# Sign bits of 27 weight chunks moved from VectorE to ScalarE and GpSimd, weight checks from step 60, two query tiles

## The chip, the cores and the metric

The kernel runs on one core of a Trainium2 chip (trn2). The engines of the core are called PE (TensorE: matmuls), DVE (VectorE), ACT (ScalarE), POOL (GpSimd) and SP (SyncE, which issues the transfers). Each engine works through its own queue of instructions in order and waits there on semaphores of the others. The metric is the time of one execution in device microseconds.

## The reference

Attention that keeps the 32 largest scores of each row, then two dense layer pairs on its output. Batch 4, 8 heads, 576 tokens, head size 64; widths 512 -> 1024 -> 512 -> 2048 -> 512.

```python
scores = scale * np.matmul(q, k.transpose(0, 1, 3, 2))
kth = np.partition(scores, -top_k, axis=-1)[..., -top_k:-top_k + 1]      # top_k = 32
scores = np.where(scores >= kth, scores, -1000000000.0)
attn = softmax(scores)                       # exp(s - max) / (sum + 1e-9)
x = (attn @ v) as [2304, 512]
...
h = x @ w_in                                 # moe_: 512 -> 1024
solu = h * softmax(h)
ln = (solu - mean) / np.sqrt(var + 1e-06) * g_ln
x2 = ln @ w_out                              # 1024 -> 512
...
h = x2 @ w_in                                # moe2_: 512 -> 2048
g = h * (1.0 / (1.0 + np.exp(-1.702 * h)))
return g @ w_out                             # 2048 -> 512
```

The weights, q, k and v come as 64-bit floating point numbers; the kernel reads them as pairs of 32-bit words.

## The kernel before, in words

Every matmul is made of three products of 16-bit parts (a value is split into a high and a low half, `PASSES`), so each operand that PE reads has been split before: ACT writes the high half, POOL or DVE the low half.

**Weights.** The four weight matrices are cut into 48 chunks of 128 x 512 (`CHUNKS`: 8 of the first matrix, 8 of the second, then alternately 4 of the third and 4 of the fourth for each of four groups g). They all live in one tile, `wt`, of 50 slots; a raw chunk takes two slots, and `w_loads` and `room` issue the next load on SP when slots ahead are free, up to 6 chunks ahead. `w_decode` (L210) makes a 32-bit float from the two words of each number with three DVE operations: L228 shifts the high word and masks it, L229 puts the sign bit back in, L230 adds the top bits of the low word. `w_split` (L255) then scales the chunk on ACT, writes the high half on ACT (L143, the helper that records every ACT operation) and the low half on POOL (L121). `DECODE` hands out 4 or 8 chunks at each of the first eight steps, in program order.

**Attention.** 72 steps, each with two heads of a block of 128 queries (18 blocks of queries come to the expert layers; there are 16 main blocks of four steps, and four tails of two). A step: `scores` on PE (L426, tile `sc`), `copy_s` on ACT, `fold` on DVE (L444 to L447), `rounds` on DVE (L455, L458: the eight largest, four times), `pick` on POOL (L468), `mask` (ACT, and POOL L476), `exp_of` and `high` on ACT, `low` on POOL (L494), `turn` (a transposing transfer on SP to the tile `et`), and three steps later `back` on PE (L577). The queries are prepared by `prep_q`, which fills one `qt` tile for each half of the heads of a block with a transposing transfer (L382) and two copies (L384); the pool holds three such tiles.

**Expert layers.** Each finished block goes through class `Block`: `a` (L681, PE, 24 matmuls), exponentials and normalisation into `zh`, `b` (L748), `x2_high` on ACT and `x2_low` on DVE (L764), and then for g = 0 to 3: `c` (L778, PE, into the one PSUM bank `m`), `tanh` (ACT, tile `t`), `gelu` (DVE, L787), `g_high` (ACT), `g_low` (POOL, L798), `d` (L805, PE, into the one PSUM bank `o`); at last `store` copies `o` to `y` on ACT. `t`, `y` and the `junk` tile of the weight checks share one pool tag with two buffers.

**Checks.** Sums of squares of all inputs are collected in `insq`; those of the weights are taken by `w_check` (L918, an ACT Square with a sum, one of 24 at each step from step `W_CHECK` = 20 on). Near the end of the program text `insq` is summed over the partitions on POOL (L1088, a custom instruction), and a flag made of all checks decides whether a slower exact version runs.

**Order.** The program text gives priorities. The order in which each engine's queue stands is made by a scheduler before the run, which puts instructions of later text ahead where it takes an engine to be free. So a change at one place moves instructions at others.

Of the kernel before, what the change touches and what calls it, by code (L numbers as in the profile page):

```python
# [1 line left out]

# [5 lines left out]
F32 = mybir.dt.float32  # L8
# [14 lines left out]
W_RAW = 6  # L23
W_STAGE = 4
TWO_BANKS = 32
LAG = 3
DECODE = (4, 4, 4, 4, 8, 8, 8, 8)
SLOTS = {6: 2, 7: 2}
FIRST_SLOT = 6
R_BUFS, EH_BUFS, QT_BUFS, GH_BUFS = 2, 2, 3, 3  # L30
TAIL_AT = (1,)
W_CHECK = 20
PIN_TO = -1
KV_BUFS, RAW_BUFS, S_BUFS, ET_BUFS = 4, 2, 3, 2
S_IN = 2.0 ** 8
S_EXP = 2.0 ** -19
S_Z = 2.0 ** 10
# [4 lines left out]
def attn_moe_kernel(tc: tile.TileContext, *args):  # L42

    nc = tc.nc
    with ExitStack() as ctx:
        flag = layers(ctx, tc, True, *args)
        again = nc.values_load(flag, min_val=0, max_val=1)
    with tc.If(again > 0):
        with ExitStack() as ctx:
            layers(ctx, tc, False, *args)  # L50


def in_order(tc, start, engines):
# [12 lines left out]
def layers(ctx, tc, quick, q, k, v, w1, w2, g_ln, w3, w4, out):  # L66
# [127 lines left out]
    def w_load(i):  # L194
# [8 lines left out]
        else:  # L203
            wraw[i] = []
            for z in range(2):
                t = ghp.tile([128, 256, 2], I32, tag="gh", name="wraw")
                nc.sync.dma_start(t.rearrange("p n a -> p (n a)"), words[:, z * 512:(z + 1) * 512])
                wraw[i].append(t)

    def w_decode(i):  # L210

        parts = wraw.pop(i)
        if not quick:
            f = wt[:, i + 1, :]
        else:
            at_f[i] = room(i + 1, 1, 0)
            f = wt[:, at_f[i], :]
            del at_raw[i]
        wraw[-1 - i] = f
        w = 512 // len(parts)  # L220
        for z, raw in enumerate(parts):
            lo, hi = raw[:, :, 0], raw[:, :, 1]
            fi = f[:, z * w:(z + 1) * w].bitcast(I32)
            ti = fi
            if quick:
                ti = (p_m.tile([128, 512], I32, tag="m", name="wi") if i % 2 and i < TWO_BANKS else
                      p_o.tile([128, 512], I32, tag="o", name="wi"))
            nc.vector.tensor_scalar(ti, hi, 3, 0x3FFFFFF8, op0=ALU.logical_shift_left, op1=ALU.bitwise_and)  # L228
            nc.vector.scalar_tensor_tensor(ti, hi, -0x40000000, ti, op0=ALU.bitwise_and, op1=ALU.bitwise_or)  # L229
            nc.vector.scalar_tensor_tensor(fi, lo, 29, ti, op0=ALU.logical_shift_right, op1=ALU.bitwise_or)  # L230
        if quick:
            return
        j, kc, cb = CHUNKS[i]
        if j == 1:
            act(f, f, AF.Copy, scale=gl[:, kc:kc + 1])
        junk = at.tile([128, 512], F32, tag="t", name="junk")
        act(junk, f, AF.Square, accum_out=wsq[:, i:i + 1])
# [17 lines left out]
    def w_split(i):  # L255
        j, kc, cb = CHUNKS[i]
        o = wview(i)
        if not quick:
            scale = wsc[:, j:j + 1]
        elif j == 1:  # L260
            scale = gl[:, kc:kc + 1]
        else:
            scale = S_W[j]
        split(wraw.pop(-1 - i), o[:, 0], o[:, 1], scale, "w")

    def w1v(kc, hl, half):
# [150 lines left out]
    def scores(blk, j):  # L417
        t = qt[blk][0]
        sc = p_sc.tile([128, 1536], F32, tag="sc", name="sc")
        for i in range(2):  # L420
            c0 = 0
            for c1 in ((MAIN, S) if i == 0 else (2 * MAIN - S, S)):
                for hl in range(2):
                    for rows, qi, kp, par in heads(blk, j, i):
                        k0 = par * 704
                        nc.tensor.matmul(sc[rows, i * S + c0:i * S + c1], t[qi // 4][:, hl, qi % 4, rows],  # L426
                                         kts[kp][:, k0 + c0:k0 + c1], start=(hl == 0), stop=(hl == 1))
                c0 = c1
        fr[(blk, j)] = [sc]

    def copy_s(blk, j):
        sc = fr[(blk, j)][0]
        s = sp.tile([128, 2, S], F32, tag="s", name="s")
        act(s.rearrange("p a n -> p (a n)"), sc[:, 0:2 * S])
        fr[(blk, j)].append(s)
# [42 lines left out]
    def exp_of(blk, j, i):  # L478
        s, pk = fr[(blk, j)]
        if j == 0 and i == 0:  # L480
            rsum[blk] = sm.tile([128, 8], F32, tag="rsum", name="rsum")
        rs = rsum[blk][:, 2 * j + i:2 * j + i + 1]
        act(s[:, i], s[:, i], AF.Exp, bias=pk[:, i, 1:2], scale=S_EXP, accum_out=rs)

    def high(blk, j):
        s = fr[(blk, j)][0]
        eh = ehp.tile([128, 2, 2 * S], F16, tag="eh", name="eh")
        act(eh[:, 0], s.rearrange("p a n -> p (a n)"))
        fr[(blk, j)] = [s, eh]
# [178 lines left out]
    class Block:  # L668
# [39 lines left out]

        def square(self):
            st_ = self.st  # L710
            self.zh = one.tile([128, 1024], F16, tag="zh", name="zh")
            self.dev = zsq[:, self.no:self.no + 1] if quick else st_[:, 5:6]
            act(self.zh, self.hf, AF.Square, bias=st_[:, 4:5], accum_out=self.dev)

# [213 lines left out]
    def w_loads(i, most=99):  # L928

        while wload[0] < min(WCH, i + 1 + W_RAW, most):  # L930
            j = wload[0]
            r = room(j, 2, max(1, min(W_STAGE, (WCH + SHIFT - j - 2) // 2)))
            if r is None:
                return
            at_raw[j] = r
            w_load(j)
            wload[0] += 1


    def decode(n):  # L940
        for _ in range(n):
            i = wnext[0]
            if i == WCH:
                return
            wnext[0] += 1
            w_decode(i)
            w_split(i)
            w_loads(i)


    last_kv = {}
# [21 lines left out]
    def load_for(t):  # L973
        for w in work.get(t, ()):
            gen = w[2](*w[3])
            next(gen)
            loaded.append(gen)
# [17 lines left out]

    def place(name):
        for f in slot.get(name, ()):
            f()

    t = 0  # L1000
    while True:
        count = 0 if t < FIRST_SLOT else SLOTS.get(t, 1)
        live = t < NS
        for z in range(max(count, 1)):
            slot = {}
            if z < count:
                place_no = len(at_step)
                at_step.append(t)
                while len(base) < len(queue) and (not base or place_no >= base[-1] + 5):
                    base.append(place_no - 1)  # L1010
                for m, b0 in enumerate(base):
                    for name, f in queue[m].at(place_no - b0).items():
                        slot.setdefault(name, []).append(f)
            on = live and z == 0
            if z == 0:
                if t + 1 < NS:
                    scores(*steps[t + 1])
                load_for(t + 1)
                if 1 <= t <= NS:
                    exp_of(*steps[t - 1], 0)  # L1020
                    exp_of(*steps[t - 1], 1)
                    high(*steps[t - 1])
                if t + 1 < NS:
                    copy_s(*steps[t + 1])
                if 1 <= t <= NS:
                    low(*steps[t - 1], 0)
                    low(*steps[t - 1], 1)
                    turn(*steps[t - 1])
                if LAG <= t < NS + LAG:
                    back(*steps[t - LAG])  # L1030
            place("gh")
            place("c")
            place("early")
            if on:
                rounds(*steps[t], (0,))
            place("dve1")
            if on:
                rounds(*steps[t], (1,))
            place("dve2")
            place("tanh")  # L1040
            if on:
                rounds(*steps[t], (2, 3))
                pick(*steps[t])
            place("dve3")
            place("gl")
            place("mid")
            if on:
                mask(*steps[t])
            place("big")
            place("d")  # L1050
            if z == 0 and t + 1 < NS:
                fold(*steps[t + 1])
            place("gelu")
            if z == 0 and LAG <= t < NS + LAG and ends(t - LAG):
                finish(steps[t - LAG][0])
            place("last")
            place("late")
            if z < count - 1 and t < len(DECODE):
                decode(DECODE[t] // count)
        if live:  # L1060
            for w in work.get(t, ()):
                run(loaded.pop(0))
            if t < len(DECODE):
                decode(DECODE[t] - (DECODE[t] // max(count, 1)) * (max(count, 1) - 1))
            if t >= W_CHECK and t - W_CHECK < WCH // 2:
                w_check(t - W_CHECK)
        t += 1
        if t == PIN_TO:
            in_order(tc, start, ("DVE",))
        if len(base) == NBLK and len(at_step) > base[-1] + 13:  # L1070
            break
# [59 lines left out]
```

## Time and profile before

| what | value |
|---|---|
| median of 3 runs | 989.79 us (986.56 to 990.15) |
| profiled execution, its own time | 986.16 us |
| its span, first to last instruction | 984.3 us |
| granted TensorE clock, mean | 0.913 |
| busy: PE, DVE, ACT, POOL | 760.7, 777.0, 709.7, 667.2 us |

No engine is busy for the whole span, since the parts of the program have different limits; the profile is best read by stretches of time. "Idle before" in a row is the time that the engine did nothing ahead of the instruction, and the name behind the arrow is what ended that; "issue" means that the profile shows nothing that it waited for.

### The profile page before, as it was taken

What the parts mean: (1) busy time and instruction counts of PE and PEld (TensorE: products, weight loads), DVE (VectorE), ACT (ScalarE), POOL (GpSimd) and SP (SyncE); (2) the same over time, 40 slices, a digit from 0 to 9 for tenths busy, and PEclk for the clock granted to TensorE, in tenths of its full rate; (3) what the DMA queues carried; (4) which work ended last, traced back from release to release, by engine and by line L of the source; (5) the groups of instructions that cost most, each with busy time, mean ns of one, the idle gap of its engine ahead of it and who ended that gap; (6) DMA issues with size and microseconds to landing.
All of it is one profiled execution on the core that took longest, in us unless ns stands there. A gap on an engine that the chain in (4) does not pass through costs nothing. (4 is left out here: it accounts for less than half of the span.)

```text
span 984.3 us, 22216 instructions
## 1 busy us (share of the span) xinstructions
PE 760.7 (77%) x8224; PEld 490.6 (50%) x8224; DVE 777.0 (79%) x2197; ACT 709.7 (72%) x1230; POOL 667.2 (68%) x673
## 2 busy tenths in 40 slices
PE   1223434644849999998899999898879999999995
PEld 0112222422525766665565665575546666666563
DVE  4999999989887898897887998798769999621220
ACT  4688777678877888889899977879478777722321
POOL 1477767659786588777788886878588877733311
PEclk9995657867778999999899999999979999999998
DMA  6998757567864477667686666757555745642200
GB/s 156 284 290 196 193 130 183 113 135 153 195 133 89 82 130 129 102 124 137 118 140 132 107 123 114 146 120 121 107 102 104 130 86 93 105 68 33 43 23 16
DMA packets 337734, 122.67 MB, mean 125 GB/s; under 512 B 315344, under 2 KB 329168, under 8 KB 337616
## 3 DMA queue, kind: packets, MB, share of 16 engines
q1 hardware_dynamic: 337616, 121.16, 59.9%
q8 instruction: 66, 1.08, 0.4%
q14 instruction: 52, 0.43, 0.1%
HBM read 39.85 MB, written 4.72 MB: 45 GB/s over the span
## 5 line engine op out<-in xcount | busy, mean ns | idle before, releaser
L455 DVE MAX8 wk<-wk 128x8 f32<-128x296 f32 x576 | 240.6, 455 | 0.0
L778 PE MATMUL h<-x2t,wt 128*128 128x128 f16 x3456 | 209.7, 221 | 14.1 <-ACT wt L143 4.6
L494 POOL TENSOR_TENSOR eh<-s,eh 128x576 f16<-128x576 f32 x144 | 181.3, 1281 | 51.9 <-ACT eh L143 32.9
L778 PEld LDWEIGHTS <-wt 128*128 128x128 f16 x3456 | 199.7, 99 | 21.9 <-issue 6.3
L476 POOL TENSOR_TENSOR s<-s,r 128x576 f32<-128x576 f32 x144 | 181.7, 1281 | 42.0 <-ACT r L143 41.8
L805 PE MATMUL o<-wt,gh 128*128 128x512 f16 x864 | 202.3, 383 | 5.7 <-DVE wt L230 3.7
L458 DVE MATCH_REPLACE8 wk<-wk 128x296 f32<-128x296 f32 x432 | 192.0, 451 | 0.0
L577 PE MATMUL av<-vt,et 128*128 128x64 f16 (+1 forms) x2400 | 91.7, 204 | 90.9 <-DMA et<-eh 82.8
L426 PE MATMUL sc<-kt,qt 128*128 128x64 f16 (+7 forms) x640 | 97.9, 320 | 76.2 <-DVE wk L447 52.7
L577 PEld LDWEIGHTS <-et 128*128 128x128 f16 (+1 forms) x2400 | 83.4, 108 | 106.1 <-DMA et<-eh 95.9
L805 PEld LDWEIGHTS <-gh 128*128 128x128 f16 x864 | 83.3, 99 | 100.1 <-issue 10.5
L798 POOL TENSOR_TENSOR gh<-t,gh 128x512 f16<-128x512 f32 x72 | 83.4, 1160 | 71.6 <-ACT gh L143 70.9
L143 ACT ACTIVATE r<-s,picks 128x576 bf16<-128x576 f32 x144 | 103.5, 765 | 31.9 <-POOL picks L468 31.5
L143 ACT ACTIVATE s<-s,picks 128x576 f32<-128x576 f32 x144 | 110.4, 767 | 22.1 <-POOL s L476 21.9
L787 DVE SCALAR_TENSOR_TENSOR t<-t,h 128x512 f32<-128x512 f32 x72 | 48.7, 677 | 90.6 <-ACT t L143 90.2
L748 PE MATMUL x<-wt,zt 128*128 128x512 f16 x432 | 105.8, 399 | 15.4 <-DMA zt<-zh 14.9
L426 PEld LDWEIGHTS <-qt 128*128 128x128 f16 (+1 forms) x640 | 48.4, 109 | 125.7 <-DVE wk L447 42.1
L681 PE MATMUL ha<-wt,xt 128*128 128x512 f16 x432 | 102.6, 396 | 10.3 <-DVE x2hl L764 10.3
L143 ACT ACTIVATE s<-sc 128x1152 f32<-128x1152 f32 x72 | 80.3, 1116 | 17.7 <-PE sc L426 12.7
L143 ACT ACTIVATE t<-h 128x512 f32<-128x512 f32 x72 | 42.1, 585 | 65.2 <-PE h L778 60.0
L143 ACT ACTIVATE eh<-s 128x1152 f16<-128x1152 f32 x72 | 83.1, 1154 | 0.7
L444 DVE TENSOR_TENSOR wk<-sc,s 128x576 f32<-128x576 f32 x72 | 54.1, 751 | 34.3 <-ACT s L143 30.3
(79 smaller groups left out, 1043.7 us busy)
## 6 DMA issues: line engine op xcount, KB each, us to landing
wt<-in_moe_w_in_dram SPq DMA_DIRECT2D x24, 512.0 KB, 5.2
wt<-in_moe_w_out_dram SPq DMA_DIRECT2D x24, 512.0 KB, 4.6
qt<-qt SPq DMA_DIRECT2D x72, 64.0 KB, 2.0
raw<-in_k_dram SPq DMA_DIRECT2D x32, 128.0 KB, 2.8
raw<-in_q_dram SPq DMA_DIRECT2D x16, 256.0 KB, 3.3
vraw<-in_v_dram SPq DMA_DIRECT2D x32, 128.0 KB, 2.6
out_dram<-y SPq DMA_DIRECT2D x16, 256.0 KB, 2.4
et<-eh SPq DMA_TRANSPOSE x72, 4.8
```

The lines of the kernel that those rows point to most:

```text
L143: nc.scalar.activation(out, in_, func, **kw)
L426: nc.tensor.matmul(sc[rows, i * S + c0:i * S + c1], t[qi // 4][:, hl, qi % 4, rows], kts[kp][:, k0 + c0:k0 + c1], start=(hl == 0), stop=(h ...
L455: nc.vector.max(out=wk[:, i, at_:at_ + 8], in_=wk[:, i, 0:W_END])
L458: nc.vector.match_replace(out=wk[:, i, 0:W_END], in_to_replace=wk[:, i, at_:at_ + 8], in_values=wk[:, i, 0:W_END], imm_value=LOW)
L476: nc.gpsimd.tensor_tensor(s[:, i], s[:, i], r[i], op=ALU.subtract)
L494: nc.gpsimd.tensor_tensor(eh[:, 1, cols], s[:, i], eh[:, 0, cols], op=ALU.subtract)
L577: nc.tensor.matmul(o[rows, col:col + 64], et[:, ea, 4 * i + c, rows], vts[kp][:, va, vc:vc + 64], start=(n == 0), stop=(n == 14))
L681: nc.tensor.matmul(h[:, half * 512:half * 512 + 512], self.xt[:, a, kc], w1v(kc, w, half), start=(n == 0), stop=(n == 11))
L748: nc.tensor.matmul(self.x2, self.zt[:, a, kc], w2v(kc, w), start=(n == 0), stop=(n == 23))
L778: nc.tensor.matmul(h2[:, mm * 128:(mm + 1) * 128], w3v(kc, w, 4 * g + mm), self.x2t[:, a, kc], start=(n == 0), stop=(n == 11))
L798: nc.gpsimd.tensor_tensor(gh[:, 1], t.rearrange("p (a n) -> p a n", a=4), gh[:, 0], op=ALU.subtract)
L805: nc.tensor.matmul(self.o, gh[:, a, mm], w4v(4 * g + mm, w), start=(g == 0 and n == 0), stop=(g == 3 and n == 11))
```

## The change

- Of the 40 chunks of the first, third and fourth matrix, two of three (27: those whose number is not 2 modulo 3) are decoded differently (`signed`). DVE shifts the high word and flips a bit in one operation, L229 is left out, and L230 follows. ACT takes the Sign of the raw high word into the slot of the chunk's high half; in `w_split` ACT's scaling copy becomes an Abs with the same scale, and POOL multiplies the result by the sign. The split into halves follows as before.
- The weight checks start at step 60 and go on after the last attention step.
- The pool of query tiles has two buffers in place of three. `zh` takes the buffer of `xt` in place of one of its own. The 4 KB per partition that this frees are not used.
- `HP_W`, `HP_MOE`, `HP_AT` and `DELAY` are new switches, all 0: `urgent` then does nothing.

```diff
+HP_W = 0
+SIGNED = (1, 1, 0)
+HP_MOE = 0
+DELAY = 0
+HP_AT = 0
...
-R_BUFS, EH_BUFS, QT_BUFS, GH_BUFS = 2, 2, 3, 3
+R_BUFS = 2
+EH_BUFS = 2
+QT_BUFS = 2
+GH_BUFS = 3
...
-W_CHECK = 20
+W_CHECK = 60
...
+def urgent(tc, offset):
+    return tc.high_priority(offset) if offset else nullcontext()
...
+    def signed(i):
+        return quick and CHUNKS[i][0] != 1 and SIGNED[i % len(SIGNED)]
...
-            nc.vector.tensor_scalar(ti, hi, 3, 0x3FFFFFF8, op0=ALU.logical_shift_left, op1=ALU.bitwise_and)
-            nc.vector.scalar_tensor_tensor(ti, hi, -0x40000000, ti, op0=ALU.bitwise_and, op1=ALU.bitwise_or)
+            if signed(i):
+                nc.vector.tensor_scalar(ti, hi, 3, -0x40000000, op0=ALU.logical_shift_left, op1=ALU.bitwise_xor)
+                act(wview(i)[:, 0], hi.bitcast(F32), AF.Sign)
+            else:
+                nc.vector.tensor_scalar(ti, hi, 3, 0x3FFFFFF8, op0=ALU.logical_shift_left, op1=ALU.bitwise_and)
+                nc.vector.scalar_tensor_tensor(ti, hi, -0x40000000, ti, op0=ALU.bitwise_and, op1=ALU.bitwise_or)
             nc.vector.scalar_tensor_tensor(fi, lo, 29, ti, op0=ALU.logical_shift_right, op1=ALU.bitwise_or)
...
+        elif not signed(i):
+            scale = S_W[j]
         else:
-            scale = S_W[j]
+            f = wraw[-1 - i]
+            act(f, f, AF.Abs, scale=S_W[j])
+            nc.gpsimd.tensor_tensor(f, f, o[:, 0], op=ALU.mult)
+            scale = None
         split(wraw.pop(-1 - i), o[:, 0], o[:, 1], scale, "w")
...
-            self.zh = one.tile([128, 1024], F16, tag="zh", name="zh")
+            self.zh = one.tile([128, 1024], F16, tag="xt", name="zh")
...
-            if t >= W_CHECK and t - W_CHECK < WCH // 2:
-                w_check(t - W_CHECK)
+        if W_CHECK <= t < W_CHECK + WCH // 2:
+            w_check(t - W_CHECK)
```

DVE's queue early in the program, where chunks 2 and 3 are decoded between the rounds of the first attention steps (L228 to L230 are the three decode operations), before:

```order
L228 TENSOR_SCALAR wi<-wt 128x512
L455 MAX wk<-wk 128x8 x2
L228 TENSOR_SCALAR wi<-wt 128x512
L229 SCALAR_TENSOR_TENSOR wi<-wt,wi 128x512
L458 MATCH_REPLACE wk<-wk 128x296 x2
L229 SCALAR_TENSOR_TENSOR wi<-wt,wi 128x512
L230 SCALAR_TENSOR_TENSOR wt<-wt,wi 128x512
```

The same place of the changed kernel, where L246 is the new first operation of a signed chunk and L249, L250 and L251 are the old three under new line numbers:

```order
L249 TENSOR_SCALAR wi<-wt 128x512
L481 MAX wk<-wk 128x8 x2
L246 TENSOR_SCALAR wi<-wt 128x512
L250 SCALAR_TENSOR_TENSOR wi<-wt,wi 128x512
L484 MATCH_REPLACE wk<-wk 128x296 x2
L251 SCALAR_TENSOR_TENSOR wt<-wt,wi 128x512 x2
```

Chunk 3 has two operations in place of three, and both chunks are finished one row earlier, ahead of what came between. Over the whole queue the last L230 stands behind 21 folds (L444) before and behind 19 in the changed kernel.

POOL's queue around the all-reduce of `insq` (L1088, with the rows marked ISA around it), before, where g_low of some block in the middle of attention comes ahead of it and a pick behind it:

```order
L476 TENSOR_TENSOR s_9152<-s_9152,r_9425 128x576
L798 TENSOR_TENSOR gh_9448<-t_9411,gh_9448 128x512
L1088 ISA
L1088 ISA tot_13436<-insq_75 128x56
L468 ISA
L468 TENSOR_TENSOR picks_73<-wk_9442,pickc_74 128x6
L121 TENSOR_TENSOR vt_10015<-vraw_9684,vt_10015 128x640
```

The all-reduce of the changed kernel (L1117 there, and L824 is g_low):

```order
L824 TENSOR_TENSOR gh_13079<-t_13037,gh_13079 128x512
L824 TENSOR_TENSOR gh_13153<-t_13134,gh_13153 128x512
L1117 ISA
L1117 ISA tot_13463<-insq_75 128x56
L824 ISA
L824 TENSOR_TENSOR gh_13222<-t_13206,gh_13222 128x512
L824 TENSOR_TENSOR gh_13291<-t_13275,gh_13291 128x512
L824 TENSOR_TENSOR gh_13362<-t_13345,gh_13362 128x512
L824 TENSOR_TENSOR gh_13429<-t_13413,gh_13429 128x512
```

It has moved from the middle of attention to the place ahead of the last four g_low of the program, those of the last block.

ACT's queue at the end of the program, before (`t` is a tanh, `gh` a g_high, `y` the copy of a block's output):

```order
L143 ACTIVATE t_13111<-h2_13060 128x512
L143 ACTIVATE gh_13130<-t_13111 128x512
L143 ACTIVATE t_13181<-h2_13132 128x512
L143 ACTIVATE gh_13197<-t_13181 128x512
L143 ACTIVATE t_13248<-h2_13199 128x512
L143 ACTIVATE y_13315,ysum_78<-o_13044 128x512
L143 ACTIVATE gh_13264<-t_13248 128x512
```

The same place of the changed kernel:

```order
L157 ACTIVATE t_13134<-h2_13083 128x512
L157 ACTIVATE junk_13154,insq_75<-wt_121 128x1024
L157 ACTIVATE gh_13153<-t_13134 128x512
L157 ACTIVATE t_13206<-h2_13157 128x512
L157 ACTIVATE junk_13223,insq_75<-wt_121 128x1024
L157 ACTIVATE gh_13222<-t_13206 128x512
L157 ACTIVATE t_13275<-h2_13226 128x512
L157 ACTIVATE y_13342,ysum_78<-o_13065 128x512
L157 ACTIVATE gh_13291<-t_13275 128x512
```

The last two weight checks (`junk`) stand between the tanh and the g_high of two groups; `junk_13223` is the last of all. Of the two buffers of their tag, `t_13206` and `y_13342` have the same one, and `junk_13223` and `t_13275` the other.

## Rows read from the trace of the kernel before

**Rows 1.** Stretches: us, busy us (x instructions) by engine, PE clock, DMA share, GB/s.

```profile
core 0: us, PE busy (x) PEld busy (x) DVE busy (x) ACT busy (x) POOL busy (x), PEclk, DMA share, GB/s
50.00:150.00 100.00, 33.29 (x370) 20.52 (x367) 98.89 (x254) 77.31 (x133) 75.19 (x75) 0.66 0.77 203
150.00:300.00 150.00, 84.99 (x760) 51.96 (x761) 135.27 (x365) 116.92 (x205) 113.44 (x114) 0.76 0.69 149
300.00:600.00 300.00, 284.06 (x3287) 186.11 (x3286) 262.48 (x785) 259.77 (x455) 231.92 (x232) 0.99 0.63 117
...
700.00:750.00 50.00, 38.63 (x467) 25.10 (x465) 36.08 (x107) 35.82 (x62) 30.91 (x33) 0.90 0.53 100
...
850.00:950.00 100.00, 97.56 (x977) 63.61 (x974) 23.42 (x54) 33.05 (x56) 33.67 (x34) 1.00 0.27 48
```

**Rows 2.** Tile wi: ns min/median/max of one, first and last start in us.

```profile
L230 DVE SCALAR_TENSOR_TENSOR wt<-wt,wi x48: 649/675/687, 12.2 to 294.6; 128x512 int32<-128x512 int32 x48
```

**Rows 3.** Timeline of POOL: start us, us, instruction, idle before.

```profile
700.08 1.16 POOL L798 TENSOR_TENSOR gh<-t,gh 128x512 f16<-128x512 f32 x1
708.10 0.68 POOL L1088 PARTITION_ALL_REDUCE tot<-insq  x1 [6.86 <-issue]
715.92 0.20 POOL L468 TENSOR_TENSOR picks<-wk,pickc 128x6 f32<-128x6 f32 x1 [7.14 <-issue]
```

**Rows 4.** Timelines of ACT, DVE and PE near 720, and of PE at 876.

```profile
716.15 1.44 ACT L143 ACTIVATE r<-s,picks 128x576 bf16<-128x576 f32 x2 [9.41 <-POOL picks L468]
...
720.19 0.69 DVE L764 SCALAR_TENSOR_TENSOR x2hl<-x,x2hl 128x512 f16<-128x512 f32 x1 [8.73 <-ACT x2hl L143]
...
720.94 6.76 PE L681 MATMUL ha<-wt,xt 128*128 128x512 f16 x24 [10.30 <-DVE x2hl L764]
...
876.82 5.34 PE L681 MATMUL ha<-wt,xt 128*128 128x512 f16 x24
```

**Rows 5.** Groups by line: form, xcount, busy us, mean ns of one, idle before.

```profile
L121 POOL TENSOR_TENSOR wt<-wt 128x512 f16<-128x512 f32 x48 | 55.3, 1160 | 22.3 <-ACT wt L143 22.1
...
L143 ACT ACTIVATE wt<-wt 128x512 f32<-128x512 f32 (+1 forms) x88 | 52.9, 618 | 2.8 <-DVE wt L230 2.3
...
L229 DVE SCALAR_TENSOR_TENSOR wi<-wt,wi 128x512 int32<-128x512 int32 x48 | 32.3, 682 | 0.1
...
L143 ACT ACTIVATE junk<-wt 128x1024 f16<-128x1024 f16 x24 | 25.1, 1047 | 0.1
...
L143 ACT ACTIVATION_READ_ACCUMULATOR junk<-wt 128x1 f32 x24 | 4.6, 192 | 0.0
```

**Rows 6.** The same stretches for line L229 alone: DVE busy (x).

```profile
0.00:50.00 50.00, 4.81 (x7) 1.00 0.84 223
50.00:150.00 100.00, 15.33 (x23) 0.66 0.77 203
150.00:300.00 150.00, 12.21 (x18) 0.76 0.69 149
```

**Rows 7.** Timeline of SP's queue: issue of the last weight load.

```profile
289.19 0.53 SPq L201 DMA_DIRECT2D wt<-in_moe_w_out_dram  x1
```

**Rows 8.** Timelines of POOL, ACT and PE in the last 40 us.

```profile
946.46 1.15 POOL L798 TENSOR_TENSOR gh<-t,gh 128x512 f16<-128x512 f32 x1 [7.04 <-ACT gh L143]
953.88 1.15 POOL L798 TENSOR_TENSOR gh<-t,gh 128x512 f16<-128x512 f32 x1 [6.28 <-ACT gh L143]
...
951.83 0.60 ACT L143 ACTIVATE t<-h 128x512 f32<-128x512 f32 x1 [5.45 <-PE h L778]
...
957.36 2.75 PE L805 MATMUL o<-wt,gh 128*128 128x512 f16 x12 [1.32 <-ACT y L143]
```

**Rows 9.** SP's waits: who for whom, us in total, times, longest.

```profile
SPq L382 <- PE sc L426: 21.4, 4, 8.1
```

**Rows 10.** Line L798: ns min/median/max of one, first and last start.

```profile
L798 POOL TENSOR_TENSOR gh<-t,gh x72: 1144/1158/1203, 179.6 to 970.2; 128x512 f16<-128x512 f32 x72
```

More of the change, by code (lines that the diff above doesn't have):

```diff
@@ L1 @@
-from contextlib import ExitStack
+from contextlib import ExitStack, nullcontext
 import concourse.bass as bass
@@ L29 @@
 FIRST_SLOT = 6
-R_BUFS, EH_BUFS, QT_BUFS, GH_BUFS = 2, 2, 3, 3
+R_BUFS = 2
+EH_BUFS = 2
+QT_BUFS = 2
+GH_BUFS = 3
+ET_BUFS = 2
+S_BUFS = 3
 TAIL_AT = (1,)
-W_CHECK = 20
+W_CHECK = 60
 PIN_TO = -1
-KV_BUFS, RAW_BUFS, S_BUFS, ET_BUFS = 4, 2, 3, 2
+KV_BUFS, RAW_BUFS = 4, 2
 S_IN = 2.0 ** 8
@@ L945, in decode @@
             wnext[0] += 1
-            w_decode(i)
-            w_split(i)
-            w_loads(i)
+            with urgent(tc, HP_W):
+                w_decode(i)
+                w_split(i)
+                w_loads(i)
     last_kv = {}
@@ L997, in place @@
         for f in slot.get(name, ()):
-            f()
+            with urgent(tc, HP_MOE):
+                f()
     t = 0
@@ L1008, in layers @@
                 at_step.append(t)
-                while len(base) < len(queue) and (not base or place_no >= base[-1] + 5):
-                    base.append(place_no - 1)
+                while len(base) < len(queue) and (not base or place_no >= base[-1] + 5 - DELAY):
+                    base.append(place_no - 1 + DELAY)
                 for m, b0 in enumerate(base):
@@ L1015, in layers @@
             if z == 0:
[L1016 to L1030, printed above, removed]
+              with urgent(tc, HP_AT):
+                  if t + 1 < NS:
+                      scores(*steps[t + 1])
+                  load_for(t + 1)
+                  if 1 <= t <= NS:
+                      exp_of(*steps[t - 1], 0)
+                      exp_of(*steps[t - 1], 1)
+                      high(*steps[t - 1])
+                  if t + 1 < NS:
+                      copy_s(*steps[t + 1])
+                  if 1 <= t <= NS:
+                      low(*steps[t - 1], 0)
+                      low(*steps[t - 1], 1)
+                      turn(*steps[t - 1])
+                  if LAG <= t < NS + LAG:
+                      back(*steps[t - LAG])
             place("gh")
```

## The prediction

> **What bounds the kernel now.** I read the stretches first [rows 1]. The first 300 us are VectorE's (DVE's): it is busy 98.9 of 100 us from 50 to 150 and 135.3 of 150 from 150 to 300, while TensorE (PE) works 33.3 and 85.0 us there. From 300 on it is PE: 284.1 of 300 us, and 97.6 of 100 from 850 to 950, where attention is over and DVE has 23.4 us of work. The border is the end of the weight decoding: its third operation (L230) runs for the last time at 294.6 [rows 2], and no block of the expert layers can finish before the last chunk is there. So there are two ways to a gain: what DVE sheds before 295 brings the PE-bound part forward by as much, and every idle stretch of PE behind 300 that goes is a gain by itself. The largest of those is in 700 to 750, where PE is busy for only 38.6 of 50 us [rows 1].
>
> That hole comes from GpSimd (POOL). The all-reduce of the input checks (L1088) takes 0.68 us, but POOL does nothing for 6.86 us before it and for 7.14 us behind it, both put down to issue [rows 3]: a stop of 14.7 us from 701.2 to 715.9. ScalarE (ACT) waits 9.41 us for the pick that is queued behind it, the copy of x2 stands behind that in ACT's queue, DVE waits 8.73 us for this copy, and PE 10.30 us for DVE [rows 4]. The 24 matmuls after it take 6.76 us, where 24 of the same kind elsewhere take 5.34 [rows 4]; the granted clock of 700 to 750 is 0.90 [rows 1], so some ran at the lower of the two levels (1.2 instead of 2.4 GHz): 1.4 us more.
>
> **Part 1: the sign of 27 chunks.** Each loses one DVE operation, L229, which fills 32.3/48 = 0.673 us [rows 5]: 27 x 0.673 = 18.2 us. Each gains a Sign on ACT, whose nearest row is the 128x512 activation on wt at 0.62 us, and a multiply on POOL, nearest the 128x512 subtraction on wt at 1.16 us [rows 5]; Abs takes the place of the scaling copy. Together ACT gets 27 x 0.62 = 16.7 us more and POOL 27 x 1.16 = 31.3. Sign needs no second table: the order has one table load as before.
>
> Where does this land? L229 ran 7, 23 and 18 times in 0 to 50, 50 to 150 and 150 to 300 [rows 6]; in chunk numbers these are 0-6, 7-29 and 30-47, with 5, 10 and 12 signed ones. POOL's work becomes 75.2 + 11.6 = 86.8 us for a stretch that would shrink to 100 - 6.7 = 93.3 us (93%), then 113.4 + 13.9 = 127.4 for 141.9 us (90%). ACT comes to 89% and 88%. None is over 100%, so DVE keeps the pace, but the slack is thin: the queues run in order, and a signed chunk now goes ACT, POOL, ACT, POOL where it went ACT, POOL. The bounds are 18.2 us (nothing lost) and 0 (all lost in new waits). For the value between them I take the row in which DVE already waits for others: in 150 to 300, with POOL at 76%, it idles 9.8% of the time; half of that share in the 93 us before, where it hardly idles now, is 4.6 us. The last chunks are short of room: the load of the last is issued at 289.19 [rows 7] and DVE decodes what has just landed, so the longer way of chunks 43, 45 and 46 counts there; I add 1.4 us. That leaves 18.2 - 6.0 = **12.2 us gained**. It carries through to the end because PE's order behind the decoding is nearly the old one, with the last chunk behind 19 folds on DVE where it was behind 21.
>
> **Part 2: the weight checks.** The 24 checks (1.05 + 0.19 us each, 29.7 us of ACT [rows 5]) leave steps 20 to 43. In 300 to 600 PE idles 15.9 us in all [rows 1] and much of that is not for ACT: the bounds are 0 and 6 us, I take 1 gained. They reappear from step 60 on, 14 of them in the drain, each ahead of a g_high; between a tanh (951.83) and the product with its result (957.36) lie 5.5 us [rows 8], so this is hidden; it costs 0 to 4, I take 1. These two cancel.
>
> More matters what hangs on them. The all-reduce reads insq, which the last check now completes almost at the end. Its place on POOL moves from the middle of attention to just before the last four g_low (L798). In the middle this **gains 10.3 + 1.4 = 11.7 us**; the bounds are 0, if another wait fills the hole, and POOL's whole 14.7.
>
> At the end it costs. By the old times [rows 8] the g_low before it ends at 947.6; 6.86 us of nothing lead to 954.5. The last check follows the tanh of 951.83 and is done at 953.7, so it is not what is late. The reduction ends at 955.2, 7.14 us of nothing at 962.3, and only then comes g_low of the last block's first group, done at 963.5 where it was 955.0. Queued behind it are the other three g_low. ACT stops too: the block output y now takes the buffer of that group's t, so it waits for this g_low (with the check rotating through the same two buffers); behind y stand g_high of the next group and the last two tanh. PE's next product may not start before y has emptied its bank: about 964.4 instead of 957.36. That is 7.0 us, and as PE idles for some 8 us there, I add 1.4 for the clock as above: **8.4 us lost**. The bounds are 0 and 14.7.
>
> The 7.14 us behind the reduction are more than half of this price. The Trainium skill (GPSIMD Engine Reference, section "Instruction dispatch") states about 6 us for the first call to a freshly loaded kernel, without a visible instruction, and nothing for the way back; by the page alone the drain would cost about 1.3 us and the sum would be 964. The row has idle time on both sides, so I keep both.
>
> **Part 3: two query tiles, one tile for xt and zh, the switches that are 0.** I cost these at 0. The third query tile let the first half of the next block's queries in early; with two it waits until the first two steps of the running block have read theirs, still two steps before it is needed. xt of the next block follows zh of this one in program order anyway. What hides a wait here is SP's queue having room; if it has none, the transposes of the exponentials behind are late, and PE with them (rival 3).
>
> **Sum**, against the profiled execution's 986.16: -12.2 - 11.7 + 8.4 = -15.5, so 970.7. The median of the three runs shown is 989.79, 3.6 above this profile; I add half of that and forecast **973**.
>
> **Rivals.** 1. More is gained: DVE loses nothing, 18.2 us, and half of the drain's 8.4 is hidden: 986.2 - 18.2 - 11.7 + 4.2 = 960.5. For it: DVE hardly waits from 50 to 150 today. Against: POOL at 93%.
> 2. POOL and ACT take the pace of the decoding and part 1 gives nothing: 986.2 - 11.7 + 8.4 = 982.9. For it: the shares above. Against: neither has more work than the time holds.
> 3. Slower: SP waits on the query tiles. Already the transpose to qt waits 21.4 us in 4 waits for PE's scores [rows 9], 5.4 each. 15 main blocks follow the first; if each waited that long in addition and a third of it reached PE, that is 27 us: 970.7 + 27 = 998. It decides from 24/15 = 1.6 us of PE per block. Against: all this is hidden where PE has other work in its queue.
> 4. The added POOL multiplies hold up DVE: 27 x 1.16 = 31 us, so 1002. Against: POOL's 128x512 subtraction takes 1144/1158/1203 ns from 179.6 to 970.2 [rows 10], though DVE is busy nine tenths of the time before 850 and a quarter behind, so no such exclusion shows. The Trainium skill (SBUF — State Buffer, section "Who interferes with whom") has one port pair that VectorE and GpSimd take in turn; by it, rival 4 would hold; this trace shows no stretching.
>
> **Chances.** My forecast 0.52, own range 965 to 981; rival 1 0.20; rival 2 0.18; rival 3 0.08; rival 4 0.02. About 0.5%, 5 us, is what a measurement of this kernel can tell from no change: faster means below 984.8, slower above 994.7. Rival 2 falls half on either side of 984.8, so faster is 0.52 + 0.20 + 0.09 = 0.81; slower is most of rival 3 and rival 4, 0.08; the rest, 0.11, is the same. The range of 957 to 988 leaves out rivals 3 and 4 and the outer half of rival 1, 2 in 10 at most.
>
> **What the profile of after would show.** L229's 27 missing operations and the last L230-like operation at 265 to 282 instead of 294.6. DVE's idle time in 50 to 150 near 5 us; 10 or more says POOL or ACT has the pace. POOL without the 14.7 us stop near 700, and PE without a gap of 10 there. The stop in the last 45 us, with a PE gap of about 8 us before the last block's first L805. I am wrong if a signed chunk's Sign or multiply blocks ACT or POOL for longer than the row of its kind; if PE gaps named after qt appear; or if the hole at 700 only moves to another wait.

## The result, and the profile after

The changed kernel takes 977.16 us (median of 6 runs, 976.35 to 980.63), the kernel before 987.41 beside it (6 runs): ratio 0.9895, 95% interval 0.9876 to 0.9915, so 8 to 12 us less. The forecast was 973, its range 957 to 988. The profiled execution took 977.06 us, span 975.3. One of the six executions of run e3 below took 4323.42 us; its median is that of the other five.

First the stretches of the changed kernel, in the columns of [rows 1]:

```profile
50.00:150.00 100.00, 35.56 (x367) 21.13 (x368) 96.22 (x244) 84.99 (x149) 88.62 (x87) 0.77 0.78 202
150.00:300.00 150.00, 95.88 (x942) 62.41 (x941) 139.50 (x371) 118.19 (x205) 127.37 (x125) 0.82 0.68 136
300.00:600.00 300.00, 281.08 (x3244) 186.84 (x3242) 265.97 (x790) 242.06 (x419) 240.26 (x243) 0.98 0.65 124
700.00:750.00 50.00, 45.59 (x520) 29.66 (x519) 44.60 (x131) 44.10 (x79) 42.43 (x40) 0.93 0.69 112
850.00:950.00 100.00, 91.36 (x838) 57.73 (x836) 19.99 (x43) 36.08 (x66) 25.77 (x26) 0.97 0.21 43
```

DVE idles 3.8 us in 50 to 150 (near 5 were forecast) and POOL is busy for 88.6 us there (93% of a shorter stretch was forecast). PE does 10.9 us more in 150 to 300 and 7.0 more in 700 to 750, and 6.2 less in 850 to 950, where the drain now stands.

The last decode operation, L251 now, by the view of its line, answers to [rows 2]: 266.4 where it was 294.6.

```profile
L251 DVE SCALAR_TENSOR_TENSOR wt<-wt,wi x48: 630/672/689, 10.9 to 266.4; 128x512 int32<-128x512 int32 x48
```

Groups by line, as in [rows 5]: 27 more instructions on wt on ACT (115 for 88), POOL's 27 new multiplies (L288), and DVE's new first operation (L246).

```profile
L157 ACT ACTIVATE wt<-wt 128x512 f16<-128x512 f32 (+1 forms) x115 | 68.5, 627 | 26.2 <-DVE wt L251 11.1 <-DMA wt<-in_moe_w_in_dram 10.8 <-POOL wt L288 4.0
...
L288 POOL TENSOR_TENSOR wt<-wt 128x512 f32<-128x512 f32 x27 | 31.3, 1161 | 23.6 <-ACT wt L157 23.5
L246 DVE TENSOR_SCALAR wi<-wt 128x512 int32<-128x512 int32 x27 | 18.4, 681 | 1.0 <-DMA wt<-in_moe_w_in_dram 0.9
```

The drain, timelines of POOL, ACT and PE of the changed kernel; they answer to [rows 3] and [rows 8]. PE's row at 727.38 stands where the hole of [rows 4] was.

```profile
936.93 0.68 POOL L1117 PARTITION_ALL_REDUCE tot<-insq  x1 [5.85 <-ACT gh L157]
944.59 1.14 POOL L824 TENSOR_TENSOR gh<-t,gh 128x512 f16<-128x512 f32 x1 [6.98 <-issue]
...
945.76 0.60 ACT L157 ACTIVATE y<-o 128x512 f32<-128x512 f32 x1 [5.63 <-POOL gh L824]
...
727.38 0.91 PE L804 MATMUL h<-x2t,wt 128*128 128x128 f16 x7 [4.41 <-DVE t L813]
...
946.50 4.65 PE L831 MATMUL o<-wt,gh 128*128 128x512 f16 x12 [7.07 <-ACT y L157]
...
953.67 2.75 PE L831 MATMUL o<-wt,gh 128*128 128x512 f16 x12
```

Read it from PE upwards: the product at 946.50 waited 7.07 us for y; y waited 5.63 us for g_low; and g_low stood behind the reduction and 6.98 us in which POOL shows nothing. The 12 matmuls then take 4.65 us, where the same 12 at 953.67 take 2.75. The granted clock is 0.57 from 946.5 to 951.0 and 1.00 from 953 to 957, so these 1.9 us are the price of the lower level (1.2 instead of 2.4 GHz).

### The profile page after: what moved, and what is told of

It is laid out like the page before. It is cut to its first block, busy times and chain, and to the rows that moved or that the text cites. A ratio compares the mean times of both kernels' runs of the same rounds, so it can differ in the third digit from the quotient of the medians.

```text
span 975.3 us, 22249 instructions
## 1 busy us (share of the span) xinstructions
PE 761.6 (78%) x8224; PEld 498.0 (51%) x8224; DVE 771.0 (79%) x2170; ACT 721.1 (74%) x1257; POOL 696.6 (71%) x700
## 4 chain that ended last, share of the span: by engine, by line
POOL 21%; ACT 17%; PE 16%; DVE 15%; DMA 15%; issue 10%; SPq 5%; ACTq 0%; POOLq 0%; DVEq 0%
PE h L804 5%; POOL s L502 5%; PE o L831 5%; ACT s L157 5%; POOL eh L520 4%; DVE wk L481 4%; DVE wk L484 4%; DMA raw<-in_k_dram 3%; PE x L774 3%; POOL gh L824 2%; ACT r L157 2%; POOL e L768 2%; POOL wt L135 2%; POOL kq L135 2%; DMA vraw<-in_v_dram 2%
## 5 line engine op out<-in xcount | busy, mean ns | idle before, releaser
L804 PE MATMUL h<-x2t,wt 128*128 128x128 f16 x3456 | 218.0, 225 | 23.4 <-DVE t L813 14.6
L804 PEld LDWEIGHTS <-wt 128*128 128x128 f16 x3456 | 207.4, 101 | 30.1 <-issue 13.4
L824 POOL TENSOR_TENSOR gh<-t,gh 128x512 f16<-128x512 f32 x72 | 83.4, 1159 | 80.5 <-ACT gh L157 73.5
L831 PEld LDWEIGHTS <-gh 128*128 128x128 f16 x864 | 83.9, 99 | 102.9 <-issue 11.3
L813 DVE SCALAR_TENSOR_TENSOR t<-t,h 128x512 f32<-128x512 f32 x72 | 48.6, 675 | 83.5 <-ACT t L157 81.5
L774 PE MATMUL x<-wt,zt 128*128 128x512 f16 x432 | 102.8, 392 | 14.8 <-DMA zt<-zh 13.2
L707 PE MATMUL ha<-wt,xt 128*128 128x512 f16 x432 | 100.6, 391 | 10.3 <-DMA xt<-xhl 9.4
L157 ACT ACTIVATE wt<-wt 128x512 f16<-128x512 f32 (+1 forms) x115 | 68.5, 627 | 26.2 <-DVE wt L251 11.1
```

What stands on the lines that cost most here:

```text
L157: nc.scalar.activation(out, in_, func, **kw)
L707: nc.tensor.matmul(h[:, half * 512:half * 512 + 512], self.xt[:, a, kc], w1v(kc, w, half), start=(n == 0), stop=(n == 11))
L774: nc.tensor.matmul(self.x2, self.zt[:, a, kc], w2v(kc, w), start=(n == 0), stop=(n == 23))
L804: nc.tensor.matmul(h2[:, mm * 128:(mm + 1) * 128], w3v(kc, w, 4 * g + mm), self.x2t[:, a, kc], start=(n == 0), stop=(n == 11))
L824: nc.gpsimd.tensor_tensor(gh[:, 1], t.rearrange("p (a n) -> p a n", a=4), gh[:, 0], op=ALU.subtract)
L831: nc.tensor.matmul(self.o, gh[:, a, mm], w4v(4 * g + mm, w), start=(g == 0 and n == 0), stop=(g == 3 and n == 11))
```

## Experiments

All against the kernel before on the same chip, whose median was 988.98, 988.91 and 988.29 us for the three groups of four runs. Each ratio is to it. The three groups (e1 to e4, e5 to e8, e9 to e12) ran on three chips, and the kernel before that was measured beside the changed kernel took 987.41. So the changed kernel is known against e4, e6 and e7 only to some 3 us: the medians put it 8.7 us above e4, 4.9 below e6 and 5.5 above e7, the ratios 9.0, 2.3 and 7.0.

| run | sign | checks from | query tiles, zh | sum of checks | median us | ratio (95%) |
|---|---|---|---|---|---|---|
| e1 | 27 | 20 | 3, own | POOL | 983.92 | 0.9955 (0.9936 to 0.9973) |
| e2 | 0 | 60 | 3, own | POOL | 985.41 | 0.9972 (0.9956 to 0.9989) |
| e3 | 0 | 20 | 2, shared | POOL | 983.08 | 0.9941 (0.9919 to 0.9963) |
| e4 | 27 | 60 | 2, shared | PE | 968.51 | 0.9804 (0.9776 to 0.9832) |
| e5 | 0 | 20 | 3, own | PE | 979.58 | 0.9911 (0.9881 to 0.9940) |
| e6 | 0 | 60 | 2, shared | POOL | 982.05 | 0.9918 (0.9891 to 0.9946) |
| e7 | 27 | 60 | 3, own | POOL | 971.70 | 0.9824 (0.9798 to 0.9851) |
| e8 | 0 | 20 | 2, own | POOL | 984.35 | 0.9949 (0.9931 to 0.9968) |
| e9 | 27 | 20 | 3, own | PE | 974.76 | 0.9869 (0.9841 to 0.9896) |
| e10 | 0 | 60 | 3, own | PE | 976.38 | 0.9879 (0.9856 to 0.9902) |
| e11 | 27 | 60 | 3, own | PE | 963.96 | 0.9746 (0.9723 to 0.9770) |
| e12 | 0 | 22 | 3, own | POOL | 990.51 | 1.0022 (1.0004 to 1.0040) |

### The three parts alone (e1, e2, e3)

Each is the changed kernel with two of its three parts set back. e1 keeps the sign:

```diff
-QT_BUFS = 2
+QT_BUFS = 3
...
-W_CHECK = 60
+W_CHECK = 20
...
-            self.zh = one.tile([128, 1024], F16, tag="xt", name="zh")
+            self.zh = one.tile([128, 1024], F16, tag="zh", name="zh")
```

e2 keeps the late checks; `QT_BUFS` and `zh` are as in e1, `W_CHECK` stays at 60, and

```diff
-SIGNED = (1, 1, 0)
+SIGNED = (0, 0, 0)
```

e3 keeps the buffers, with `SIGNED` as in e2 and `W_CHECK` as in e1.

> The changed kernel with the weight checks back at step 20, three query tiles and zh in a buffer of its own: the sign of 27 chunks alone. My theory: the shorter decoding gives 12 us (end of decoding near 266 us instead of 294.6), and POOL's stop at the all-reduce stays in the middle of attention: 987.4 - 12 = 975 us, with a PE gap of about 10 us near 700. Rival A (all of the gain came with the all-reduce, and the decoding gave back to ACT and POOL what DVE saved): 987 us. Rival B (the drain loses to the checks on ACT, not to the all-reduce) says the same as my theory here.

> The changed kernel with no chunk signed, three query tiles and zh in its own buffer: only the weight checks start at step 60. My theory: 11.7 us gained where the stop in the middle goes, 8.4 lost where it stands in the drain: 984 us, decoding ending near 295 us, a PE gap of 7 to 8 us before the last block's first product with the fourth matrix. Rival A: 977 us. Rival B: 984 us as well, but the gap in the drain is then spread over the checks.

> The changed kernel with no chunk signed and the checks back at step 20: only two query tiles and the tile shared by xt and zh. My theory: 987 us, within 2. Rival C (SP's queue waits on the query tiles, and this is what the changed kernel lost of the forecast gain): 990 us or more, with PE waiting for transfers of qt.

The checks came out as forecast (985.4 for 984). The other two did not: the sign gave 5 us, nearer to rival A, and the buffers, costed at 0, gave 5 to 6. In e1 the decoding ends just as early as in the changed kernel, at 266.3, and yet attention is no earlier. The 31st pick by the view of its tile (first and last start, counted up to it), of before and of e1:

```profile
L468 POOL TENSOR_TENSOR picks<-wk,pickc x31: 185/195/218, 30.7 to 404.1; 128x6 f32<-128x6 f32 x31
```

```profile
L494 POOL TENSOR_TENSOR picks<-wk,pickc x31: 188/201/215, 30.7 to 405.0; 128x6 f32<-128x6 f32 x31
```

So the 28 us on the decoding are not 28 us, nor 12, at this pick. (It is one pick of 72; the last starts at 850.8 before and 843.6 in e1.)

### The sum of the checks on TensorE (e4, e5)

The all-reduce gives way to one matmul with a tile of ones, in e4 in the changed kernel, in e5 in the kernel before:

```diff
+        ones = cst.tile([128, 128], F32, name="ones")
+        nc.vector.memset(ones, 1.0)
...
-    tot = sm.tile([128, insq.shape[1]], F32, tag="tot", name="tot")
-    nc.gpsimd.partition_all_reduce(tot, insq, channels=128, reduce_op=bass_isa.ReduceOp.add)
+    tot = p_m.tile([128, 512], F32, tag="m", name="tot")[:, 0:insq.shape[1]]
+    nc.tensor.matmul(tot, ones, insq, start=True, stop=True)
```

> The changed kernel with the sum over the partitions of insq taken by one matmul with a tile of ones on TensorE, in place of POOL's all-reduce; the checks on ACT stay where they are. My theory: POOL has no stop in the drain, the PE gap of 7.1 us there goes: 977.2 - 8.4 = 969 us. Rival B (the checks on ACT make the drain longer): 976 to 977 us, and the gap ahead of the last block stays.

> The kernel before, with one thing changed: the sum of the checks over the partitions is made by one matmul with a tile of ones on TensorE in place of GpSimd's all-reduce. Nothing else moves, so this run prices the stop in the middle alone. Theory (part 2 of the prediction: 10.3 + 1.4 = 11.7 us): about 977 us where before takes about 988.5, no POOL stop near 700 and no PE gap of 10 us near 720. Rival: the steps of attention set the pace there and the lead is lost again in later waits: 983 to 986, though the gap is gone. The run of the checks alone (985.4, 3 us under before) is bare of a verdict here, since it holds a gain in the middle and a loss at the end.

Both are near the theory, e5 at 979.58 with 2.4 us less gain than its 11.7. e4 is 8.7 us under the changed kernel (968.51 for 977.16). PE's timeline in e4's drain shows the same product with a wait of 1.32 us, as in [rows 8], and the sum itself at 0.32:

```profile
938.79 2.75 PE L833 MATMUL o<-wt,gh 128*128 128x512 f16 x12 [1.32 <-ACT y L159]
...
951.92 0.32 PE L1119 MATMUL tot<-insq,ones 128*128 128x56 f32 x2
```

e5 is 9.3 us under before. Its stretches, as in [rows 1]:

```profile
700.00:750.00 50.00, 49.08 (x597) 31.37 (x594) 45.67 (x139) 41.53 (x74) 39.89 (x40) 1.00 0.64 108
750.00:850.00 100.00, 97.64 (x1124) 65.45 (x1117) 88.89 (x265) 75.22 (x125) 77.07 (x78) 1.00 0.62 105
```

PE gets 10.5 us back in 700 to 750, the clock stays at the upper level, and 1.4 of them go again in 750 to 850 (97.64, where before has 99.08).

The all-reduce of `insq` is not the only one. A second, of the one flag `bad`, stands last on POOL in every version, in e4 and e5 too; the section on the hardware has its rows.

### The parts taken out of the whole (e6, e7), and the query tiles alone (e8)

e6 is the changed kernel without the sign (`SIGNED` as in e2). e7 is the changed kernel without the buffers (`QT_BUFS` and `zh` as in e1). e8 is e3 with a buffer of its own for `zh`, so of all parts only this is left:

```diff
-QT_BUFS = 3
+QT_BUFS = 2
```

> The changed kernel without its part 1 (no chunk has its sign made by ACT and POOL), so checks from step 60, two query tiles and zh in xt's buffer stay. What part 1 is worth beside the other two: after takes 977. Theory that part 1 was mis-sized whatever stands beside it (alone it gave 4.5 us): 981 to 982. Rival A, that part 1 is worth its 12.2 us once the stop in the middle is gone (the early lead ran into that stop when it stood alone): 988 to 990. Rival B, that parts 2 and 3 already give what there is (alone 2.8 and 5.8) and the sign adds almost nothing: 977 to 979. In every case the last decode operation is near 296 instead of 266.

> The changed kernel without its part 3: three query tiles and a buffer of its own for zh; the sign and the late checks stay. Theory that part 3's 5.8 us, measured alone, carry into the whole: 983. Rival A, that part 3 is worth 0 here as the prediction costed it, and that its 5.8 us alone came from another order of the queues around the stop in the middle, which the late checks take away anyway: 976 to 978. From the single parts, sign and checks add up to 7.3 us less than before, 981.

> The kernel before with two query tiles instead of three and nothing else: zh keeps its own buffer, the checks stay at step 20, no sign is moved. With both buffer edits the time was 983.7, 5 to 6 us under before. If the query tiles (later query loads, so another order on SP and the engines) are the cause: 983 to 985. If it is zh's shared buffer: 988 to 990. If rival 3 of the prediction has something in it, the SP waits, it is above 990 and PE gaps are named after qt.

e8 is at 984.35 and e3 at 983.08: what the buffers do comes from the query tiles. e6 says that beside the late checks and the buffers the sign is worth 4.9 us (982.05 to 977.16), or 2.3 by the ratios. e7 came out as no theory had it: without the buffers the changed kernel is 5.5 us faster (7.0 by the ratios). Sign and checks together take off 17.2 us (988.91 to 971.70), where alone they take 5.1 and 3.6. Two surprises, then: the sign is worth much more beside the late checks, if the buffers are not there; and the same two query tiles gain 5 us alone and cost 5 beside the rest.

For the second, the stretches of e7, then of e8, then one of e6, beside those of the changed kernel above and of before in [rows 1]:

```profile
150.00:300.00 150.00, 93.78 (x912) 59.25 (x910) 130.57 (x375) 116.62 (x204) 128.49 (x129) 0.78 0.67 140
700.00:750.00 50.00, 48.92 (x578) 31.14 (x576) 46.93 (x140) 41.41 (x71) 39.70 (x40) 1.00 0.60 116
```

```profile
150.00:300.00 150.00, 89.39 (x848) 57.01 (x847) 140.49 (x387) 114.12 (x196) 111.87 (x114) 0.76 0.69 146
700.00:750.00 50.00, 42.32 (x456) 26.77 (x455) 40.13 (x124) 35.87 (x61) 35.19 (x35) 0.93 0.55 101
```

```profile
150.00:300.00 150.00, 89.35 (x850) 56.42 (x849) 140.75 (x388) 112.16 (x192) 110.60 (x114) 0.76 0.70 146
```

With two query tiles DVE idles less from 150 to 300 (busy 140.49 for 135.27 of before) and 88 more matmuls (848 for 760) are done there. With the sign there is less of that to win: 942 for 912. In 700 to 750 the two tiles cost: PE is busy for 45.59 us in the changed kernel at a clock of 0.93, for 48.92 at 1.00 in e7. PE's gap of 4.41 us at 727.38, above, lies there; e6 and e4, with two tiles too, have gaps of 4.4 and 4.0 us at the same instruction, while e5, e7, e9, e10 and e11, with three, have none over 1.6 us from 700 to 790. What PE waits for is a gelu on DVE (L813). The rows ahead of it in the changed kernel:

```profile
719.96 1.73 PE L804 MATMUL h<-x2t,wt 128*128 128x128 f16 x28
724.66 0.58 ACT L157 ACTIVATE t<-h 128x512 f32<-128x512 f32 x1
726.67 0.66 DVE L813 SCALAR_TENSOR_TENSOR t<-t,h 128x512 f32<-128x512 f32 x1
```

The tanh starts 3.0 us after these matmuls have ended and the gelu 1.4 us after the tanh has. Neither engine idles before it; both work through attention that their queues have ahead. No transfer stands in this chain.

### The sign and the checks apart (e9, e10, e11), and a control (e12)

All three with three query tiles, zh's own buffer and the sum on TensorE as in e4, so that the stop around the sum of the checks is nowhere: the sign alone, the checks alone, both. e12 is the kernel before with one number changed:

```diff
-W_CHECK = 20
+W_CHECK = 22
```

> The sign of 27 chunks alone (three query tiles, zh's own buffer, checks from step 20), with the sum of the checks made by a matmul on TensorE, so that the stop in the middle is gone too. Part 1 gave 4.5 us alone (984) and about 14 beside the late checks (971.7 against 985.4). What made the difference? Theory A, the stop: the lead from the decoding ran into POOL's stop near 700, which stood in the way of whatever was early; then the sign is worth 12 to 14 beside the TensorE sum (979.6 without the sign): 966 to 968. Theory B, ACT: with the checks in steps 20 to 43, ACT has no room for attention to follow the earlier decoding, so the lead is lost between 300 and 550 and the stop has no part in it: 974 to 976, and the steps of attention (pick 30) no earlier than before, as in the run of the sign alone.

> Part 2 alone (checks from step 60; no sign, three query tiles, zh's own buffer) with the TensorE sum. Beside the same sum with checks at step 20 (979.6) this is what leaving steps 20 to 43 and standing in steps 60 on is worth by itself, without the all-reduce anywhere. The prediction had 1 gained and 1 lost: 979 to 980. Rival, ACT is what the middle waits for even without the sign: 974 to 977. Beside the run of the checks with the all-reduce (985.4) it prices the reduction in the drain once more: 8.4 us by the prediction, so 977, between the two.

> The changed kernel without its two buffer edits and with the TensorE sum: the candidate for the best version. The run without the buffers took 971.7; the sum on TensorE took 8.7 us off the changed kernel. If the drain's price is the same here: 963. If the buffer edits' 5.5 us were a thing of the all-reduce's place: 968, as with the buffers.

> A control: the kernel before with its weight checks begun at step 22 instead of 20. No work is added or taken away, but the scheduler writes another order on every engine (some 12,900 differing lines on PE). How far does another order alone move the time? If it is an innocent thing: within 2 us of before, 987 to 990. If the order alone is worth what the two buffer edits gave (5.8 us less alone, 5.5 more beside the rest): off by 3 to 6 us in either direction, and then no single run of a changed kernel prices an edit closer than that.

From e5 at 979.58, the sign alone takes off 4.8 (e9), the late checks alone 3.2 (e10), both 15.6 (e11). So beside the late checks the sign is worth 976.38 - 963.96 = 12.4 us, beside the early ones 4.8. Theory A is out: taking away the stop doesn't make the sign worth more, taking away the early checks does. That is what theory B forecast; whether ACT's room is its cause is another question. Where the lead goes shows in the stretches from 150 to 300 and from 300 to 600, of e5 and e9 (checks early, without and with the sign), then of e10 and e11 (checks late):

```profile
150.00:300.00 150.00, 80.55 (x756) 50.97 (x757) 133.78 (x364) 115.14 (x200) 113.82 (x116) 0.75 0.71 149
300.00:600.00 300.00, 285.00 (x3290) 186.50 (x3289) 264.42 (x788) 261.86 (x459) 232.38 (x233) 0.99 0.65 118
...
150.00:300.00 150.00, 92.99 (x924) 58.63 (x922) 131.71 (x379) 118.42 (x207) 129.64 (x129) 0.79 0.68 142
300.00:600.00 300.00, 276.74 (x3185) 181.02 (x3183) 261.61 (x772) 261.22 (x457) 232.53 (x232) 0.98 0.65 119
```

```profile
150.00:300.00 150.00, 83.07 (x760) 52.87 (x761) 134.78 (x364) 116.56 (x202) 113.65 (x116) 0.75 0.70 150
300.00:600.00 300.00, 282.35 (x3280) 186.30 (x3279) 263.00 (x780) 237.84 (x409) 232.07 (x233) 0.99 0.62 117
...
150.00:300.00 150.00, 94.36 (x939) 59.28 (x938) 132.79 (x380) 118.09 (x206) 130.07 (x130) 0.80 0.68 143
300.00:600.00 300.00, 280.61 (x3242) 186.37 (x3239) 265.00 (x780) 242.06 (x417) 236.78 (x235) 0.98 0.67 122
```

From 150 to 300 PE is busy 12.4 us longer with the sign beside the early checks and 11.3 beside the late ones. From 300 to 600 it is then busy 8.3 us less in the first case and only 1.7 less in the second: the lead is lost there, or kept. The checks take 26.28 us of ACT in 300 to 600 of e9, none in e11. DVE's waits for ACT from 300 to 400, in the columns of [rows 9], of e9 and then of e11:

```profile
DVE wk L472 <- ACT s L159: 6.2, 4, 2.8
DVE st L726 <- ACT e L159: 3.2, 2, 2.8
DVE t L815 <- ACT t L159: 3.1, 3, 1.5
DVE rsum L628 <- ACT s L159: 2.0, 1, 2.0
DVE x2hl L792 <- ACT x2hl L159: 0.7, 1, 0.7
```

```profile
DVE t L815 <- ACT t L159: 5.6, 3, 2.4
DVE wk L472 <- ACT s L159: 3.4, 3, 2.9
DVE rsum L628 <- ACT s L159: 1.8, 2, 0.9
DVE st L726 <- ACT e L159: 1.2, 1, 1.2
```

The 31st pick of e9 and of e11:

```profile
L496 POOL TENSOR_TENSOR picks<-wk,pickc x31: 190/199/216, 30.9 to 406.2; 128x6 f32<-128x6 f32 x31
```

```profile
L496 POOL TENSOR_TENSOR picks<-wk,pickc x31: 189/199/214, 31.2 to 397.0; 128x6 f32<-128x6 f32 x31
```

From 300 to 400 DVE waits for ACT 12.0 us in place of 15.2, and the folds (wk) wait 2.8 us less for the copy of the scores. But from 300 to 600 DVE waits for ACT 33.6 us in e11 and 32.2 in e9, so these waits by themselves don't carry the difference.

At the 31st pick e11 is 9.2 us earlier than e9; beside the early checks the sign leaves that pick where it was (406.2, and 405.4 in e5), beside the late ones it makes it 11.7 us earlier (397.0, and 408.7 in e10). The lead at a pick isn't even, though: the 50th is at 605.8 in e9 and later, at 609.5, in e11, the last at 839.6 and 833.4. The profiled execution of e10 was 2.3 us under its median and that of e11 2.0 above, so the two traces hold 8.2 of the 12.4 us. What the runs don't tell apart is ACT's time from the order that the checks' move writes on the other engines. e10 by itself speaks against ACT's time: it lies in its rival's range (976.38), yet with the checks off ACT, PE is busy 2.7 us less than in e5 from 300 to 600 and the 31st pick is 3.3 us later.

The control is 2.2 us slower than before (0.04 to 0.4%), between the two expectations: this one other order of the queues is worth about 2 us, and a difference of that size prices no edit.

e11 is the best version: 2.5% under before, 13 us under the changed kernel by the medians.

## Why the prediction came out as it did

The direction and the range were right. Of the terms the drain held, the middle was a little too large, the sign's holds under a condition, and the buffers' was wrong.

- **Part 1, 12.2 us gained.** The durations held: POOL's multiply 1.16 us, ACT 0.627, the pace left to DVE, the last decode operation at 266.4 in the forecast 265 to 282. The 12.2 hold beside the late checks (12.4), and so do the 6.0 allowed for new waits: DVE idles 6.7 us in 50 to 150 of e11 and 17.2 in 150 to 300, where e10 has 1.4 and 15.2: 7.3 more. The step that failed is "It carries through to the end": a shorter decoding brings the rest forward only if attention, behind it, can follow, and with the checks in steps 20 to 43 it did not (4.8); by which engine is not shown. In the changed kernel, with the two query tiles, it is 4.9 (2.3 by the ratios) though the checks are late. One part of that may be that the tiles alone already bring matmuls forward into 150 to 300: the sign adds 92 there (942 for the 850 of e6), where with three tiles it adds 168 (e9 to e5) and 179 (e11 to e10); that was not tested.
- **Part 2, the relief of ACT, 1 gained and 1 lost.** Mis-sized: the late checks alone are worth 3.2 us without the reduction (e10), and 7.6 more beside the sign (15.6 - 4.8 - 3.2); that ACT's time is the reason is not shown. The sum took the parts as independent, and these two are not.
- **Part 2, the stop in the middle, 11.7 gained.** Right in mechanism, somewhat too large: 9.3 (e5), and 9.2 from e1 to e9. The gap of 10.3 goes, and some of it is lost again behind it.
- **Part 2, the stop in the drain, 8.4 lost.** Right: 8.7 (e4), 9.0 (e2 to e10), 7.7 (e7 to e11). The chain was the one written down: g_low, y by its buffer, PE's product at 946.50 with a gap of 7.07 where 7.0 was worked out, and 1.9 us for the clock, not 1.4. As worked out, nearly all of the price comes from behind the reduction (see the last section).
- **Part 3, costed at 0.** Wrong: 5.5 us lost in the changed kernel (e7), 4.5 with the TensorE sum (e11 to e4), 4.6 to 5.9 gained alone (e8, e3). "What hides a wait here is SP's queue having room" asked only for waits on the tiles. Behind 300 us PE has none named after qt in the changed kernel, and 1.6 us in all for the transposed exponentials; the 4.41 us gap is a wait for ACT and DVE. So the tile count probably reaches the time through the order that the scheduler writes; no run tests that.
- **The sum.** -15.5 was forecast. By the runs with three query tiles it is -4.8 (sign) - 3.2 (checks) - 7.6 (both at once) - 9.3 (middle) + 7.7 (drain) = -17.2. That is e7's time, split along one chain of runs, and no independent check of the terms; another order of the edits would size sign and checks otherwise. Part 3 brings it to -10.3 (7.0 by the ratios). That the total came within some 4 us of the forecast of 973 is in part luck: sign and middle fell short by 7.4 and 2.4 us, the checks beside them gave 10.8 that stood at nothing, and part 3 lost what stood at nothing too.
- **Rivals.** Rival 2 (part 1 gives nothing) is out: the sign gave 4.8 us or more wherever it was tried with three tiles. Rival 3's waits are there, but small: the waits of the transpose to qt for PE are 51.9 us in 16 (31.8 + 10.3 + 9.8 for av, h and sc) where they were 40.6 in 12, not 80 more. Rival 4's stretching doesn't show: POOL's multiplies ran at 1161 ns with DVE at 96%.

SP's waits for PE in the changed kernel, in the columns of [rows 9]:

```profile
SPq L408 <- PE av L603: 31.8, 8, 8.0
SPq L408 <- PE h L804: 10.3, 3, 8.4
SPq L408 <- PE sc L452: 9.8, 5, 2.5
```

Still open is what in attention takes the sign's lead back beside the early checks, why the kernel with two query tiles leaves PE short near 727, and how sign and buffers stand together with early checks, which was not run. With a control that moved 2 us, none of these terms is known closer than that.

## What to carry to other kernels

An engine relieved in one stage gives time only as far as the next stage can follow: look up whether the stretch behind keeps the lead or loses it again. Price two edits that load or relieve the same engine together, and run both alone and both at once; here they were worth 8.0 us one by one and 15.6 together. A count of buffers is an edit of the whole order where a scheduler writes the queues; and an all-reduce on GpSimd can cost far more idle time around it than its own, so price what stands behind it in the queue, and try whether a matmul can make the sum.

## What the runs showed of the hardware

The stop around POOL's all-reduce moves with it: 6.86 us before and 7.14 behind in the middle [rows 3], 5.85 and 6.98 in the drain, for 0.68 us of work; a matmul of 0.32 us in its place gave back 7.7 to 9.3 us.

The idle time ahead can run while POOL has nothing to do. In the drain the last check ended on ACT at 935.89 and g_high at 936.42, so the next g_low could not have started before; the reduction started at 936.93, and that g_low at 944.59, about 8 us late, nearly all of it from behind the reduction. The second all-reduce, of `bad`, also starts 5.7 to 6.2 us after POOL's last instruction in all the traces here, though its operand is there about 2 us earlier. In the best version, e11:

```profile
954.72 0.15 DVE L1127 TENSOR_SCALAR bad<-ok 128x1 f32<-128x1 f32 x1
956.91 0.38 POOL L1128 PARTITION_ALL_REDUCE bad<-bad  x1 [5.86 <-issue]
957.33 0.15 DVE L1130 TENSOR_SCALAR flag<-bad 128x1 int32<-128x1 f32 x1 [2.45 <-POOL bad L1128]
```

The 2.0 us between operand and start are in the chain that ends last, in e11 as in before (2.2); taking this reduction off POOL too was not tried.

The Trainium skill (GPSIMD Engine Reference, section "Instruction dispatch") states about 6 us for the first call to a freshly loaded kernel and nothing for the way back. The idle time ahead is of that size, though no run shows whether a kernel is loaded there; behind, both rows have about as much again, and the measurement decides. By the page alone the drain would have cost 1.3 us, an estimate; it cost 7.7 to 9.0.
